# Two ScalarE passes that convert weights: the first writes float32 into the weight's own tile instead of bfloat16 into the raw one

## Chip, cores and metric

One core of one Trainium2 chip. The metric is the device time of the core in microseconds (us); the kernel before took a median of 1000.03 us in three runs (998.05 to 1000.8).

The engines are named as in the profile: PE (TensorE matmul), PEld (its weight load), DVE (VectorE), ACT (ScalarE), POOL (GpSimd), SP (SyncE, which here issues every DMA). Each engine works through its own instructions in order.

## The reference

Pooled attention, then a gated feed-forward block over the 4608 tokens:

```python
k_p = k.reshape(B, H, S // 8, 8, D).mean(axis=3)        # B = H = 8, S = 576, D = 64
v_p = v.reshape(B, H, S // 8, 8, D).mean(axis=3)
attn = softmax(q @ k_p.T / sqrt(D))                     # 1e-9 added to each sum
x = (attn @ v_p).transpose(0, 2, 1, 3).reshape(B * S, H * D)
xn = x / sqrt(mean(x * x) + 1e-6) * rms_g
g = xn @ w_gate                                         # 512 -> 1536
out = (g * sigmoid(g) * (xn @ w_val)) @ w_out           # 1536 -> 512
```

The three weight matrices reach the kernel as 64-bit words (float64 values seen as int64), and the kernel makes float32 of them on the chip.

## The kernel before

**Shape of the work.** The tokens go in nine blocks of 512. The first three blocks are multiplied plainly (`mm1`, `mm2`; tiles `psg` and `po` in the profile); the later six go in pairs through a scheme with seven products of halves instead of eight (`pxy`, `pf`), whose weight blocks and sums of blocks were stored to DRAM (`blocks`, `sum`, `vB`, `vs`) in the first part and are loaded back for each pair. Every operand is split into a high part and a low part in fp32r, so that each product takes three matmuls. Attention for a batch (`pss` scores, `pst` turned probabilities, `psx` result) runs ahead of the block that needs it.

**Order.** One table of steps, `ORDER`, fixes the order of the instructions on all engines: a step is a name of one or two letters and its indices, `:` is followed by the PSUM banks that it takes, `/` by the numbers of the slots that it takes in a pool with several slots. Steps with an underscore belong to the first part (batches 0 and 1 and block 0). Nothing is rearranged after that.

**The conversion.** The weights come in 26 chunks, ten of 1024 words a partition and sixteen of 512. Each chunk passes these steps, whose letters stand in `ORDER`:
- `l` (`w_load`, L321): a DMA from DRAM to a raw tile `wx`, moved by three bytes, so that byte 4 of each 8 is the double's top byte (sign and seven exponent bits) and the 32-bit word at byte 0 holds the bits below it.
- `a` (`w_bend`, L327, ACT): a Prelu with a bias, which reads that byte as int8 at every eighth byte and writes bfloat16 at bytes 4 and 5 of the same eight, in `wx` itself.
- `b` (`w_top`, L336, ACT): takes the chunk's own tile `wt` (for the 512 chunks a slot of the tag `out`, 0 or 1; for the 1024 chunks a region of the weights' space), reads the bfloat16 at every eighth byte, and writes int32 densely into `wt`: the sign and the top of the exponent in float32's place. Two Prelus in a row give the function with two bends that the exponent needs.
- `c` (`w_join`, L340, DVE): shifts the word at byte 0 of each eight and ORs it into `wt`, which is then the float32 weight. It is the last reader of `wx`.
- `h` (`w_hi`, L354, ACT) rounds `wt` to the high part, `w` or `W` (`w_lo`, L305, DVE or POOL) subtracts it for the low part. This is the last reader of `wt`.

The slots `out` 0 and 1 are shared: besides the `wt` of the 512 chunks they hold the tiles that `wh` and `wl` fill (L781, L785) and `ws` stores (L789), and later results on their way out.

**Who else uses ACT at that time.** All exponentials (L451, L509), most copies from PSUM (L552, L554, L593, L600), Silu (L1047), the high parts of the activations (L1085), and a table load of 1.28 us at each change between Exp, Silu and Sqrt.

Of the kernel before, what the change touches and what calls it, by code (L numbers as in the profile page):

```python
# [15 lines left out]
BF16 = mybir.dt.bfloat16  # L16
# [59 lines left out]
_bb/1 _B01:6 _h8 _H01 _cb _m103 _u1 wf01 Wf02 _E111 _w8 _G1 _m113 _F1 wh03/0 Wl03 _la _X100 _hb _Wb _lf/0 Wf03 ws03
_e2:0 _o0:7564 _aa _g2:3 _i1/1 _ba _ca _L1 wh02/1 _o1 wl02 _af _u2 _G2 _R111 _bf/0 _cf _F2 _N110 _Q10 wd0 _i2/1
_T110:2/1 _D110 _hf _Wf _j2 _ha _g3:1 _lc _q12 _e3:0 wh01/0 _V11/0 _u3 _G3 _wa ws02 _o2 _N111 _F3 _ac _bc _cc _k13
_i3/0 _lh/0 _ah _hc _g4 _T112:1 _bh/1 _D112 _j3 _T111:3 _le _D111 _e4:0 _ch _u4 _hh wl01 ws01 Wt1/0 wh04/0 _ae Wl04
_Wc Wf10 _S12:32 _lg _Wh Wf11 Wf12 wf13 _be _M120 _M121 ws04 _G4 _F4 wh11/1 wl11 _ce _A110:1 _v20/1 _V20/1 _Y110 ws11  # L80
_o3 _A111:1 wh13/0 wd1 _i4/0 Wt2/1 _E120 _g5:0 wh14/1 _R120 Wl14 ws14 Wf20 _li Wl13 _L4 ws13 _ag _o4 _bg _e6 _he _We
Wf21 _u5 _cg _E121 _R121 wf22 _N121 wh12/1 Wl12 _e5:2 ws12 _G5 _Y111 _T121:1/1 Wf23 _F5 _i5/0 wh23/0 _v12 _j5 _N120
_D121 Wl23 wh21/1 Wl21 _q13 _K13/1 _T122 _ai _bi _ll/0 _hg ws23 ws21 _Wg _g6 _u6 _V12/0 _D122 _lk _k20 _v13 _o5 _G6
wh22/1 _F6 _i6/1 _ci _S13:10 _M130 _T120:3 wh24/0 Wl24 _D120 _j6 wl22 _M131 _g7 _u7 _hi ws22 _e7 _ak _o6 _K20/1 _bk
_ck _G7 _F7 ws24 _E130 _A121:3 _al _bl/1 _cl _ln/1 _an _bn/0 _cn _i7/1 _R130 _E131 _R131 _N131 _A120:2 _Y120 _hn _Wn
_j7 _Y121 _g8:1 _u8 _V13/0 _G8 _wi _N130 wd4 _e8:0 _F8 _hl _wl _lj/0 _aj _bj/0 _cj _lm/1 _am _bm/1 _T131:1/1 _o7 _D131
_hk _T130 _D130 _q20 sc20:21 wd2 _Q11/0 _cm _T132 _D132 _Wk _hj _A130:3 _Y130 Wt3/1 Wf30 _A131 _Y131 Wf31 lv21/0
# [169 lines left out]
def body(ctx: ExitStack, tc: tile.TileContext, qT, kT, vN, w1, w2, gain, out, outT):  # L257
# [51 lines left out]
    def w_load(n):  # L309
# [910 lines left out]
```

## Time and profile before

| what | value |
|---|---|
| median of three runs | 1000.03 us |
| profiled execution, its own time | 998.13 us |
| its span, first to last instruction | 996.4 us |
| PE busy | 956.7 us, 96% of the span |
| DVE, ACT, POOL busy | 666.6, 540.6, 482.6 us |
| conversion passes on ACT (L327, L336), all before 193 us | 26 and 26 instructions |
| DMA | 211.40 MB, mean 212 GB/s |

PE is busy nearly all the time, so the span is PE's work plus PE's idle time. The tenths of busy time in 40 slices (24.9 us each) show where the idle time lies, and the line of the granted clock where PE worked at a lower clock; the timeline of an engine tells, in brackets, how long it was idle before a piece of work and which engine, tile and line ended the wait. The chain that ended last is given to 69% to PE, 5% to POOL and 3% each to DVE, ACT and DMA.

### The profile page before, as it was taken

Reading aid. Unit: us, or ns where it says so; the run is one execution under the profiler, and the core shown is the slowest. Engines: PE = TensorE matmul, PEld = TensorE weight load, DVE = VectorE, ACT = ScalarE, POOL = GpSimd, SP = SyncE. Lnnn points to the kernel's source line nnn. Section 1 sums busy time; section 2 is a strip of 40 time slices with the busy share of each in tenths; the row PEclk is TensorE's granted clock in tenths of the full one; section 3 lists DMA queues with packets and bytes.
Section 4 is the critical chain, followed back from the end, with each engine's and each line's share of the span. In section 5 each row is a group of like instructions: output and inputs, shape, how many; then the busy total and the mean of one; then the engine's idle time right before and its main releaser. Section 6 shows DMA issues by size and latency. Waiting matters only on the chain.

```text
span 996.4 us, 14144 instructions
## 1 busy us (share of the span) xinstructions
PE 956.7 (96%) x4670; PEld 758.5 (76%) x4670; DVE 666.6 (67%) x1084; ACT 540.6 (54%) x955; POOL 482.6 (48%) x618
## 2 busy tenths in 40 slices
PE   7777988999999999999999999999999999999998
PEld 7466766877777787777777777878778778888886
DVE  6435756788889689878877868746566785442433
ACT  6899989854564655755446455541534552212332
POOL 3324543711231323442335688741276896245786
PEclk7579999999999999999999999999999999999999
DMA  9425666566667756977978776657786575766646
GB/s 290 154 99 174 232 228 183 189 203 202 199 212 216 221 146 195 302 238 230 291 223 270 217 234 219 215 188 250 237 275 188 159 235 171 219 212 206 215 142 208
DMA packets 142296, 211.40 MB, mean 212 GB/s; under 512 B 12240, under 2 KB 78288, under 8 KB 142224
## 3 DMA queue, kind: packets, MB, share of 16 engines
q1 hardware_dynamic: 142224, 210.51, 68.0%
q8 instruction: 37, 0.61, 0.3%
q14 instruction: 35, 0.29, 0.1%
HBM read 154.23 MB, written 56.23 MB: 211 GB/s over the span
## 4 chain that ended last, share of the span: by engine, by line
PE 69%; POOL 5%; DVE 3%; ACT 3%; DMA 3%; issue 1%; SPq 0%; DVEq 0%; ACTq 0%
PE pxy L905 30%; PE pf L985 14%; PE psg L1069 13%; PE po L1103 6%; PE psx L570 3%; PE pss L488 3%; POOL fp L305 2%; POOL xp L305 1%; DMA wp<-blocks 1%; ACT wx L327 1%; DMA pt<-rows 1%; DMA out<-o 1%; POOL w L305 1%; DVE xraw L654 0%; ACT wt L336 0%
## 5 line engine op out<-in xcount | busy, mean ns | idle before, releaser
L905 PE MATMUL pxy<-xp,wp 128*128 128x512 f32 x1512 | 361.2, 391 | 1.7 <-ACT o L1114 0.8
L905 PEld LDWEIGHTS pxy<-xp,wp 128*128 128x128 f32 x1512 | 282.4, 188 | 65.5 <-issue 2.9
L985 PE MATMUL pf<-fp,ring 128*128 128x512 f32 x756 | 189.6, 393 | 1.8 <-DVE fu L305 0.8
L1069 PE MATMUL psg<-xh,w 128*128 128x512 f32 x544 | 172.4, 399 | 6.8 <-ACT prob L451 6.1
L985 PEld LDWEIGHTS pf<-fp,ring 128*128 128x128 f32 x756 | 139.7, 188 | 38.0 <-issue 2.7
L1069 PEld LDWEIGHTS psg<-xh,w 128*128 128x128 f32 x544 | 101.9, 191 | 32.6 <-ACT prob L451 7.4
L1069 PE MATMUL psg<-xl,w 128*128 128x512 f32 x272 | 107.1, 394 | 0.0
L305 POOL TENSOR_TENSOR hl<-act,hh 128x256 fp32r<-128x256 f32 x58 | 46.9, 830 | 115.8 <-ACT hh L1085 94.6
L305 POOL TENSOR_TENSOR fp<-fs,fp 128x256 fp32r<-128x256 f32 x108 | 81.1, 777 | 41.0 <-ACT fp L958 37.2
L305 POOL TENSOR_TENSOR fp<-act,fp 128x256 fp32r<-128x256 f32 x72 | 55.0, 785 | 82.3 <-ACT fp L958 81.0
L305 POOL TENSOR_TENSOR w<-wt,w 128x256 fp32r<-128x256 f32 x50 | 43.2, 892 | 73.8 <-ACT w L354 73.8
L1103 PE MATMUL po<-w,hh 128*128 128x512 f32 x288 | 74.0, 394 | 0.0
L1103 PEld LDWEIGHTS po<-w,hh 128*128 128x128 f32 x288 | 55.1, 191 | 11.9
L305 POOL TENSOR_TENSOR fp<-hb,fp 128x256 fp32r<-128x256 f32 x68 | 54.5, 827 | 13.6 <-ACT fp L958 13.6
L1069 PEld LDWEIGHTS psg<-xl,w 128*128 128x128 f32 x272 | 51.7, 190 | 11.3
L1164 ACT COPY hb<-pxy 128x512 f32<-128x512 f32 x36 | 21.0, 587 | 72.1 <-PE pxy L905 72.1
L340 DVE SCALAR_TENSOR_TENSOR wt<-wx,wt 128x512 uint32<-128x512 uint32 (+1 forms) x26 | 23.5, 908 | 48.0 <-ACT wt L336 46.1
L958 ACT CAST fp<-act 128x512 fp32r<-128x512 f32 x36 | 22.2, 619 | 58.3 <-DVE act L1172 49.0
L958 ACT CAST fp<-fs 128x512 fp32r<-128x512 f32 x54 | 33.1, 618 | 34.6 <-POOL fs L305 17.5
L327 ACT ACTIVATE wx<-wx,shift 128x512 bf16<-128x512 int8 (+1 forms) x26 | 48.9, 1893 | 4.7 <-DMA wx<-w 4.7
L1171 DVE TENSOR_TENSOR u<-u,pxy 128x512 f32<-128x512 f32 x36 | 24.7, 685 | 39.7 <-PE pxy L905 39.5
L305 POOL TENSOR_TENSOR fs<-act,hb 128x256 f32<-128x256 f32 x32 | 23.3, 751 | 50.4 <-DVE act L1172 28.0
(194 smaller groups left out, 1634.0 us busy)
## 6 DMA issues: line engine op xcount, KB each, us to landing
wp<-sum SPq DMA_DIRECT2D x144, 256.0 KB
wp<-blocks SPq DMA_DIRECT2D x108, 256.0 KB
ring<-vs SPq DMA_DIRECT2D x72, 256.0 KB
ring<-vB SPq DMA_DIRECT2D x54, 256.0 KB
sum<-wt SPq DMA_DIRECT2D x48, 256.0 KB
blocks<-w SPq DMA_DIRECT2D x24, 512.0 KB
wx<-w SPq DMA_DIRECT2D x10, 1023.6 KB
v<-vN SPq DMA_DIRECT2D x32, 288.0 KB
```

The source lines that it names most:

```text
L305: getattr(eng, op)(*(x[..., o:o + step] for x in (out, a, b)))
L327: nc.scalar.activation(u, z, AF.Prelu, bias=shift[:, 0:1], alpha=SMALL)
L340: nc.vector.scalar_tensor_tensor(u, raw["x", n][0], 5, u, ALU.logical_shift_right, ALU.bitwise_or)
L488: nc.tensor.matmul(s["ps", h][:, t * SP:(t + 1) * SP], s["q"][r, o:o + P], s["pk"][r, :], start=True, stop=True)
L570: nc.tensor.matmul(ps[r, :n], s["pv"][:, r], x, start=True, stop=True)
L905: nc.tensor.matmul(ps[:, :NB], w[:, a, c, :], x[:, b, c, :], start=j == 0 and not more, stop=j == len(todo) - 1, skip_group_check=more)
L958: nc.scalar.copy(y[:, 0], f_source(i, k, j))
L985: nc.tensor.matmul(ps[c], w[:, a, c * P:(c + 1) * P], x[:, b], start=j == 0 and n == 0 and not more, stop=j == HALF - 1 and n == 2, skip_g ...
L1069: nc.tensor.matmul(ps[:, :NB], w[:, c, cols], x[c], start=(j == 0), stop=(j == len(todo) - 1))
L1103: nc.tensor.matmul(po[i][t], x[i, f][:, t * P:(t + 1) * P], w, start=(f == 0 and k == 0), stop=(f == NF - 1 and k == 2))
L1164: cp=lambda i, f: S_.copy(later(i, f), st["XY", i, f, 0]),
L1171: v1=lambda i, f: V.tensor_add(u2(i, f), u2(i, f), st["XY", i, f, 5]),
```

## The change

The first pass `w_bend` now takes the chunk's own tile `wt` and writes float32 densely into it; the second pass `w_top` reads this float32 and writes int32 in place, over it. The raw tile is only read. With the tile, the slot number (`/0`, `/1`) moves in `ORDER` from `b` to `a`, sixteen times; the table has the same 3289 steps in the same order (its lines are broken elsewhere, which is why all of it stands in the diff). The numbers of lines after the passes are smaller by five.

```diff
-_zg:6 _q00 _q02 _l5/0 _k00 _K00 _S00:16 _a5 _b5/0 _c5 _k02 _K02 _S02:24 _M001 _M000 _U001 _E000 _M021 _M020 _U021 _k01
+_zg:6 _q00 _q02 _l5/0 _k00 _K00 _S00:16 _a5/0 _b5 _c5 _k02 _K02 _S02:24 _M001 _M000 _U001 _E000 _M021 _M020 _U021 _k01
...
-        raw["x", n] = x[:, :, 0], x.bitcast(I8)[:, :, 4], x.bitcast(BF16)[:, :, 2]
+        raw["x", n] = x[:, :, 0], x.bitcast(I8)[:, :, 4]
...
     def w_bend(n):
-        _, z, u = raw["x", n]
-        nc.scalar.activation(u, z, AF.Prelu, bias=shift[:, 0:1], alpha=SMALL)
-
-    def w_top(n):
         f, j = CHUNKS[n]
         if j == 3:
             t = space2(f + 1 if f < 3 else NF - 1 - f % 2, [P, 2 * WC], F32, f"wt{n}")
         else:
             t = two([P, WC], F32, tag="out", name=f"wt{n}")
         raw["t", n] = t
-        nc.scalar.activation(t.bitcast(I32), raw["x", n][2], AF.Prelu, scale=UNIT, bias=shift[:, 1:2], alpha=1.0 / SMALL)
+        nc.scalar.activation(t, raw["x", n][1], AF.Prelu, bias=shift[:, 0:1], alpha=SMALL)
+
+    def w_top(n):
+        t = raw["t", n]
+        nc.scalar.activation(t.bitcast(I32), t, AF.Prelu, scale=UNIT, bias=shift[:, 1:2], alpha=1.0 / SMALL)
```

No instruction changes its place on any engine. What moves is the wait for `wt`'s slot: from the second pass to the first. Two places on ACT show it. The first is near 23 us, chunks 1 and 0 (L327 is the first pass, L336 before and L331 now the second). Before:

```order
L327 ACTIVATE wx_242<-wx_242,shift 128x512 [waits DMAHW4_49]
L327 ACTIVATE wx_242<-wx_242,shift 128x512 [waits DMAHW7_49]
L449 ACTIVATE early<-early 128x5 [waits DVE_49]
L451 ACTIVATE prob,early<-pss_0_0_275,early 128x72 [waits PE_49,Activation_49,Pool_49]
L451 ACTIVATE prob,early<-pss_0_0_275,early 128x72 x4
L453 ACTIVATE early<-early,tiny 128x5 [waits Activation_49]
L336 ACTIVATE wt_305<-wx_242,shift 128x512
L554 COPY own_139<-pst_2_2_309 72x2x64 [waits PE_49]
L336 ACTIVATE wt_313<-wx_242,shift 128x512 [waits Pool_49]
```

Now:

```order
L327 ACTIVATE wt_271<-wx_242,shift 128x512 [waits DMAHW4_49]
L327 ACTIVATE wt_273<-wx_242,shift 128x512 [waits DMAHW7_49,Pool_49]
L444 ACTIVATE early<-early 128x5 [waits DVE_49]
L446 ACTIVATE prob,early<-pss_0_0_277,early 128x72 [waits PE_49,Activation_49]
L446 ACTIVATE prob,early<-pss_0_0_277,early 128x72 x4
L448 ACTIVATE early<-early,tiny 128x5 [waits Activation_49]
L331 ACTIVATE wt_271<-wt_271,shift 128x512
L549 COPY own_139<-pst_2_2_310 72x2x64 [waits PE_49]
L331 ACTIVATE wt_273<-wt_273,shift 128x512
```

The wait for POOL, which ends its subtraction from the slot's last tenant, stands ahead of the exponentials now and behind them before.

The second place is near 163 us, the first passes of chunks 19 and 22, with the copies of turned probabilities (`pt`) behind them. Before:

```order
L354 CAST w_9_1372<-wt_1303 128x512 [waits DMAHW5_49,DVE_49]
L327 ACTIVATE wx_1375<-wx_1375,shift 128x512 [waits DMAHW3_49]
L336 ACTIVATE wt_1378<-wx_1375,shift 128x512 [waits Activation_49,Pool_49]
L327 ACTIVATE wx_1381<-wx_1381,shift 128x512 [waits DMAHW4_49]
L336 ACTIVATE wt_1384<-wx_1381,shift 128x512 [waits DVE_49,Activation_49]
L552 COPY pt_3_1386<-pst_3_1_1387 72x512 [waits PE_49]
```

Now:

```order
L349 CAST w_9_1372<-wt_1302 128x512 [waits DMAHW5_49,DVE_49]
L327 ACTIVATE wt_1377<-wx_1375,shift 128x512 [waits DMAHW3_49,Activation_49,Pool_49]
L331 ACTIVATE wt_1377<-wt_1377,shift 128x512 [waits Activation_49]
L327 ACTIVATE wt_1383<-wx_1381,shift 128x512 [waits DMAHW4_49,DVE_49]
L331 ACTIVATE wt_1383<-wt_1383,shift 128x512 [waits Activation_49]
L547 COPY pt_3_1386<-pst_3_1_1387 72x512 [waits PE_49]
```

Here too the waits for POOL and DVE moved up by one instruction, from the second pass of a chunk to its first.

## Rows read from the trace of the kernel before

**Rows 1.** The page: busy tenths and granted clock in 40 equal slices.

```profile
PE   7777988999999999999999999999999999999998
ACT  6899989854564655755446455541534552212332
PEclk7579999999999999999999999999999999999999
```

**Rows 2.** Busy time by stretch: us, PE, PEld, DVE, ACT, POOL, PEclk, DMA share, GB/s.

```profile
200.00:996.40 796.40, 786.88 (x3804) 626.11 (x3802) 550.02 (x891) 368.77 (x612) 397.88 (x510) 1.00 0.71 217
```

**Rows 3.** ACT's groups up to 200 us, by shape: busy us, mean ns, idle before.

```profile
L327 ACT ACTIVATE wx<-wx,shift 128x1024 bf16<-128x1024 int8 x10 | 26.1, 2607 | 0.0
L327 ACT ACTIVATE wx<-wx,shift 128x512 bf16<-128x512 int8 x16 | 22.9, 1446 | 4.7 <-DMA wx<-w 4.7
L336 ACT ACTIVATE wt<-wx,shift 128x512 int32<-128x512 bf16 x16 | 12.1, 757 | 0.5
L336 ACT ACTIVATE wt<-wx,shift 128x1024 int32<-128x1024 bf16 x10 | 12.1, 1209 | 0.3
```

**Rows 4.** ACT's timeline: start us, length us, instruction.

```profile
29.64 2.58 ACT L327 ACTIVATE wx<-wx,shift 128x1024 bf16<-128x1024 int8 x1
31.97 0.68 ACT L552 COPY own<-pst 72x512 f32<-72x512 f32 x1
...
81.55 1.19 ACT L336 ACTIVATE wt<-wx,shift 128x1024 int32<-128x1024 bf16 x1
82.64 0.61 ACT L1085 CAST hh<-act 128x512 fp32r<-128x512 f32 x1
83.15 1.45 ACT L327 ACTIVATE wx<-wx,shift 128x512 bf16<-128x512 int8 x1
84.69 0.77 ACT L336 ACTIVATE wt<-wx,shift 128x512 int32<-128x512 bf16 x1
```

**Rows 5.** Line L327 alone by stretch: us, ACT busy (count), PEclk, DMA.

```profile
20.00:41.00 21.00, 6.59 (x4) 0.50 0.58 175
41.00:56.00 15.00, 5.40 (x3) 0.73 0.50 177
...
67.00:88.30 21.30, 5.56 (x3) 0.97 0.21 78
...
119.00:130.00 11.00, 2.62 (x1) 0.99 0.85 262
130.00:135.00 5.00, 0.00 (x0) 0.68 0.54 151
135.00:160.00 25.00, 8.10 (x4) 1.00 0.70 224
```

**Rows 6.** PE's timeline where it had been idle: idle us and releaser in brackets.

```profile
32.02 1.07 PE L546 MATMUL pst<-ident,main 128*72 128x128 f32 x4 [2.16 <-POOL main L478]
...
38.40 1.23 PE L570 MATMUL psx<-own 72*64 72x288 f32 x4 [1.50 <-ACT own L552]
...
55.91 1.23 PE L570 MATMUL psx<-own 72*64 72x288 f32 x4 [5.97 <-ACT own L600]
...
88.30 1.60 PE L1103 MATMUL po<-w,hl 128*128 128x512 f32 x4 [4.60 <-ACT prob L451]
...
129.91 1.22 PE L1069 MATMUL psg<-xh,w 128*128 128x512 f32 x2 [2.38 <-ACT prob L451]
...
141.94 1.33 PE L488 MATMUL pss<-pk,q 64*128 64x72 f32 x18 [0.55 <-ACT pt L554]
...
159.87 0.73 PE L1069 MATMUL psg<-xh,w 128*128 128x512 f32 x2 [3.74 <-ACT prob L451]
```

**Rows 7.** ACT's timeline: a wait for PE, and a first pass near 163 us.

```profile
66.86 0.58 ACT L552 COPY pt<-pst 72x512 f32<-72x512 f32 x1 [1.76 <-PE pst L546]
...
163.62 1.48 ACT L327 ACTIVATE wx<-wx,shift 128x512 bf16<-128x512 int8 x1
```

**Rows 8.** POOL's timeline near 161 us: a subtraction of two pieces.

```profile
161.56 3.04 POOL L305 TENSOR_TENSOR w<-wt,w 128x256 fp32r<-128x256 f32 x2
```

More of the change, by code (lines that the diff above doesn't have):

```diff
@@ L15 @@
 U8 = mybir.dt.uint8
-BF16 = mybir.dt.bfloat16
 AF = mybir.ActivationFunctionType
@@ L234 @@
[L234 to L236 removed]
+_zg:6 _q00 _q02 _l5/0 _k00 _K00 _S00:16 _a5/0 _b5 _c5 _k02 _K02 _S02:24 _M001 _M000 _U001 _E000 _M021 _M020 _U021 _k01
+_O021 _K01 _f _k03 _v03 _V03 _I021 _K03 _R000 _O001 _q01 _I001 _h5 _N000 _N001 _S01:10 _M010 _k10 _M011 _U011 _E020 _N021
@@ new lines @@
+xc400 lq42 sc42:03 me26:2 gt26 rc31 whb2/0 mx420/1 sb420 wsb1 ex420 whb3/1 dm41 rs31 vl26 Wlb3 mx421/1 sb421 mo25 av401:1
+ft301 sm420/0 xd40 hi26/0 Lo26 ex421 sm421/0 Wlb2 lq43 sc43:32 mx431/0 xc401 dp41/1 av411 xd41 mx430/1 xc411 av410:1
+xc410 lv42/1 wsb3 pv42/0 Wfb3 whb4/1 mg27:0 gt27 Nm421 Nm420 Wlb4 tr42/0 sb431 ex431 lk50 pk50/1 sb430 lv43/1 pv43/1
+sm431/1 ex430 sm430/1 me27:1 zt40/1 Nm430 zt41 vl27 Nm431 me28:0 mo26 dm42 sq40 lq50 tr43/0 wsb2 hi27/1 wsb4 Zf40 Zf41
+Lo27 zh41/1 Zl41 ft311 dp42/1 Zf42 Zf43 mg28:3 sc50:12 mx501/1 dm43 zh43/0 gt28 vl28 zl43 zs43 sb501 yh31 zs41 yl31
@@ new lines @@
+ys35 yh35 zh54/1 pr310 rl315/3 Zl54 cp31 mo2b pr312 lk52 pk52/0 rl304/1 yh34 Yl34 rl302/4 ev22/0 pr302 rl321/2 lv50/1
+sb511 sa31 ex511 st22 zs54 yl32 Yl35 pr320:0 pr304:4 ev21/0 pr315:7 rl301/7 sb510 sa30 rl311/4 sm511/0 pv50/0 ev20/1
+rl313/6 ex510 rl314/0 sm510/0 Nm510 pr301:6 u230 st21 st20 ev23/0 ys36 pr303 u330 pr313:1 c230 pr311:5 rl305/1 pr305:6
+yh36 zh51/1 pr314 Yl36 rl325/5 u231 Zl51 rl333/6 pr325 u331 c231 v231 lq52 v230 pr321:4 rl316/4 Nm511 sw30 vb30 pr316
+dp50/1 sw31 vb31 rm41:1 rl306/3 v131 rt41 rl324/7 va31 pr306 v130 sc52:25 va30 Fs310 fh300/5 Fl300 rl323/4 tr51/0 cp32
@@ new lines @@
+pm321 pr386 sw38 rl396/3 vb38 Fs332 rl394/7 pr394:0 fh332/4 rs50 Fs341 v138 xc611 sa38 Nm621 ft330 rl393/4 pr393:6 u339
+c239 sw39 rl3a3/1 Fl332 tr62/0 pr395:1 v239 lq63 rl392/6 pr392 av610:7 xc610 lv63/1 sq60 Fs342 pv63/0 ft331 sc63:20
+mx631/1 va38 rl3a1/2 fh322/7 dm62 rl3a4/7 mx630/1 pm330:76 sb631 ft332 _J10 sb630 rl3a5/0 sa39 pr396 v139 va39 pm331
+ex631 Fl322 dp62/0 Fs362 sm631/0 fh323/5 rl3b2/3 fh340/8 ft322 Nm631 pr3a0:0 cp3a vb39 pr3a3:2 rl3b0/5 Fs333 ex630
+sm630/0 Fs343 pr3a1:1 fh333/6 pr3a4:3 Fl333 pm322 Fs363 sq61/0 pm332 Nm630 tr63/1 Fl323 dm63 u23a u33a c23a sw3a Fl340
@@ new lines @@
+fh342/7 pr3a5:1 v23a vb3a av620:2 pr3b0:3 cp3b rl3a2/7 pr3a2 ft334 xc620 Fs344 pr3b2 yh50 lk71 pk71/1 Jn61 ft333 pm333
+rl3a6/2 pr3a6 v13a rl3b1/6 sa3a ft323 ft324 va3a Fs334 fh334/3 av621:2 fh324/4 xd62 yh51 xc621 pm323 Fl334 rl3b3/4
+pr3b3:0 sa3b Fl342 Fl324 dp63/1 yl50 av631:1 xd63 xc631 yl51 fh343/5 av630:2 pm324 sq62/0 Jn62 pr3b1 fh351/6 rl506/1
+rl3b4/5 zs51 Fl343 u23b rl500/3 xc630 pr3b4:1 rl3b6/0 pm334 rl3b5/2 pr3b5:2 sq63/0 fh341/4 Jn63 sh6/1 u33b c23b v23b sw3b
+Fl351 Fs364 vb3b ft340 pm340:10 fh344/3 fs335 Sl6 Fl341 rl510/5 lq70 pr3b6 v13b va3b rm60:3 rt60 rc60 ft341 rs60 pm341
@@ new lines @@
+fh360/3 oe30 rl523/6 Fl354 ys56 sw50 Qd30 yh56 Yl56 qf30/0 fh362/5 rl514/3 Fl360 lv70/1 u351 pr514:4 Nm701 c251 ft354
+sw51 qf31/1 v250 pv70/1 lq71 pm354 rl515/0 pr515 v251 ft355 rl520/2 pm355 qg31 ex700 ft360 rl524/3 sm700/1 qg30 pr520:4
+Nm700 pr506 v150 cp52 rl530/7 va50 rl516/0 pr523:5 Fl362 Fl363 pr516 pm360 v151 fh500/4 tr70/0 ft361 rl525/1 rl526/6
+pr521:2 u252 vb50 u352 rl522/5 pr524:7 c252 ft362 pr522 fh361/8 Fl361 pr525 v252 sc71:75 va51 mx711/0 rl531/2 mx710/1
+pm361 rm61:2 Fl500 sb711 ex711 pm362 Fs510 fh364/7 dm70 fh510/8 sb710 pr526 v152 ex710 rl533/4 ft363 pm363 rl534/5
@@ new lines @@
+pr586 ft531 dp72/0 av720:3 v158 rl594/5 va58 pr594:7 ft530 of30 fh522/7 Fs542 pv73/1 lq73 av721:6 xc721 rl5a0/7 xd72
+sc73:10 fh532/8 rl593/1 mx731/1 pr593:6 xc720 sb731 ex731 mx730/0 sb730 ex730 Fl550 u359 c259 pr5a0:3 Fl532 Fs562 rl5a2/4
+rl5a3/6 pr5a3:1 sm730/1 fh531/6 Fl531 Fl522 pm521 rl5b4/5 sm731/1 Nm731 rl5b1/1 pr595:7 v259 pr5a1:0 sw59 vb59 cp5a
+rl596/7 pr596 v159 rl592/6 ft522 Fs533 rl5a4/7 pm522 rl5b0/0 u25a u35a pm530 pr592 pr5a2 fs561 ft532 Fs543 fh543/4 sq72/1
+Fl543 Nm730 rl5a5/2 tr73/0 dm73 sa5a ft524 pr5a4:0 fh533/7 c25a pm531 pr5a5:1 Jn72 pr5b0:3 pr5b1:0 Fl533 sa59 va59
@@ new lines @@
+rl5a6/3 pm532 ft523 ft533 v25a pr5a6 fh523/6 Fl523 pm533 sw5a vb5a cp5b Fs544 u25b Fs534 dp73/0 av730:2 fh542/8 Fl542
+fh534/5 v15a rl5b6/1 av731:1 xd73 Fs563 pm523 rl5b2/6 fh541/7 Fl541 va5a xc731 xc730 sq73/0 Jn73 Fl534 rl5b3/0 fh524/6
+pr5b3:1 u35b pr5b4:0 ft534 sh7/0 sl7 rl5b5/2 Fl524 c25b ft543 sw5b pr5b5:2 v25b vb5b fs535 rm71:1 ft542 rm70 pm524 rt71
+ft540 pr5b2 fh540/6 rc71 rt70 sa5b pm534 rc70 Fl540 ft541 Fs545 pr5b6 fh544/5 pm540:30 Fl544 v15b va5b pm541 fh525/6
+pm542 rs70 pm543 ft544 pm544 rl710/0 rs71 fh535/8 rl702/2 ys73/10 yh70 Fl525 fh551/7 ft525 pm525 Fl535 Fs565 fh545/4
@@ new lines @@
+pm710:76 rl766/2 pr766 rl762/5 pr762 ft704 rl790/4 v176 og51 sw76 rl780/3 rl781/1 Fs715 pm704 vb76 Fs730 Fs740 fh713/7
+ft712 Fl713 rl772/0 pm711 ft713 pr780:1 pr790:0 ft705 cp78 Fl712 pm712 sa76 va76 fh714/6 pr781:2 fh720/3 u278 pm713 Fl720
+rl773/6 pr772 ft714 pr773:2 pm705 rl782/3 pr782 ft715 rl784/7 fh715/8 Fl714 qa70 pm714 u377 sa77 rl774/2 pr774 ft720
+fh740/4 rl775/0 qa71 c277 pr775 v277 Fl715 pm715 qb70 Fl740 rl783/1 rl776/4 pr776 v177 sw77 vb77 rl793/2 pm720 cp79
+rl785/5 pr784 ft721 fh730/8 Fl730 va77 rl794/0 pr783:7 u378 rl792/4 Fs731 ft730 c278 qb71 sw78 Fs760 fh721/7 Fs741
@@ L237 @@
+qg70 fh761/8 fh762/5 ft761 Fl761 ft762 fh763/4 Fl763 Fl762 fh764/6 pm761 ft764 ft763 ft765 qg71 Fl764 og70 og71 oe71
+pm762 pm763 fh765/7 Fl765 pm764 of70 pm765 qh70 qh71 oh70 oh71
 """
```

293 lines of the change are left out of this document (123 added, 170 removed).

## The prediction, made before the changed kernel was run

> **What bounds the kernel now.** I read the 40 slices first. PE stands at 9 from the eighth slice to the last but one; the only sevens and eights, and the only granted clock below 9, are in the first seven slices, up to some 174 us; ACT stands at 8 and 9 in six of those seven [rows 1]. The stretch from 200 us on confirms it: PE is busy 786.88 of 796.40 us at a clock of 1.00, ACT 368.77 [rows 2]. Past 200 us the time is PE's own work and at most 9.5 us can be gained there; a change to ACT's weight conversion, which ends at 193 us, pays only as far as it closes PE's holes before 200 us.
>
> Next I read those holes from PE's timeline [rows 6]. Seven are of interest: 2.16 us before 32.02 (released by POOL), 1.50 before 38.40, 5.97 before 55.91, 4.60 before 88.30, 2.38 before 129.91, 0.55 before 141.94 and 3.74 before 159.87, these six released by ACT. Together 20.9 us, 18.7 of them ended by ACT. So ACT is the bound in that part, and the question is how much ACT time the change takes out ahead of each hole.
>
> **Part 1: the first pass (L327).** It takes 1446 ns for 512 elements and 2607 for 1024, 49 us in all for 26 instructions; the second pass, the same function with the same kind of bias, takes 757 and 1209 [rows 3]. Both read one element in every eight bytes. They differ in two things: the first reads int8 instead of bfloat16, and writes two bytes in every eight where the second writes densely. The second pass's row thus clears the stepped read of the charge, at least for two-byte elements. What is left is the stepped two-byte write, which the change removes, or the int8 read, which it keeps. No row of before shows an int8 read with a dense write, so I bound it: from above by today's 1446 and 2607 (the read is the cost, gain nothing), from below by a plain dense float32 pass, 0.61 us for 512 [rows 4]. I take the second pass's 757 and 1209, because that row has the function, the step and the dense four-byte write, and differs in the type read alone.
>
> A saving on ACT is the distance from one start to the next, not the duration. A first pass of 1024 holds the next independent instruction back by 31.97 - 29.64 = 2.33 us, a second pass by 82.64 - 81.55 = 1.09 [rows 4]; the saving is 1.24. For 512 I take off the same overlaps, 0.25 and 0.10: 1.20 against 0.66, a saving of 0.54. Where its own second pass follows at once it has to wait for the end (83.15 to 84.69 [rows 4]), and the saving is the difference of the durations, 0.69 and 1.40.
>
> The Trainium skill, ScalarE: Activation LUTs, section What ACT_TABLE_LOAD costs, says that an ACTIVATE with a bias operand takes 280 ns plus 0.833 ns for each element whatever the function, 706 ns for 512 as an estimate from that page. The second pass's 757 agrees with it, the first pass's 1446 doesn't; by the page alone the first pass would have nothing to lose, by the row it has 0.69 us to lose.
>
> **Part 2: the second pass.** It reads dense float32 instead of stepped bfloat16. Between 757 now and 0.61 us for the plain dense pass [rows 3, 4] there is at most 0.15 us to gain each; I take nothing. That it works in place costs nothing that I can see, since DVE's join and this pass keep their places in the order.
>
> **Part 3: what reaches PE.** The counts come from L327's rows by stretch [rows 5], the holes from PE's timeline [rows 6]. I carry the shift along:
> - 20 to 41 us: four first passes, three of 512 and one of 1024, 3 x 0.54 + 1.24 = 2.9 on ACT. The hole at 32.02 is ended by POOL, behind the first two only (1.1); the rest can only come out of the 1.50 before 38.40. So between 1.1 and 2.6; I take 1.9.
> - 41 to 56: three, one of 512 with its second pass behind it, one of 1024, one of 512: 0.69 + 1.24 + 0.54 = 2.5. The hole of 5.97 is larger. Shift 4.4.
> - 56 to 67: one of 1024. ACT has to wait 1.76 us for PE at 66.86 [rows 7], so this saving makes that wait longer. Nothing.
> - 67 to 88.3: two of 512, one of 1024 that ends before a table load: 0.54 + 1.40 + 0.69 = 2.6, less than the hole of 4.60. Shift 7.0.
> - 88.3 to 130: PE works through from 88.30 to 127.5, so only what lies close to the hole counts. One of 1024 (1.40) runs in the last eleven us. The hole is 2.38; with what earlier passes leave over I take 2.0. Shift 9.0.
> - 135 to 160: two of 1024 and two of 512, all with their second passes behind them: 2 x 1.40 + 2 x 0.69 = 4.2, against holes of 0.55 + 3.74 = 4.3. Shift 13.2.
> - 160 to 200: four of 512, no hole of PE behind them. Nothing.
>
> **Part 4: the wait that moves.** The first pass now needs the slot `out` that the second needed before. ACT works in order, so behind a first pass that waits stand the copies and exponentials for PE. The worst place that the rows show is chunk 19's: POOL subtracts from the slot's last tenant until 161.56 + 3.04 = 164.60 and the first pass starts at 163.62 [rows 7, 8]. It would wait 1.0 us, about as much as it and its neighbour save; PE has no ACT hole there, and I charge 0.2.
>
> **Part 5: the clock.** After the 2.38 us hole two matmuls took 1.22 us, after the 3.74 us hole another two 0.73 [rows 6], and in the 5 us from 130 the granted clock was 0.68 [rows 5], between the levels 1.2 and 2.4 GHz: 5 x 0.32 = 1.6 us of work lost. If that hole and the last one close, 0 to 3.2 us come on top (an estimate from that one row, twice). I leave it out of the sum and put it into the range.
>
> **The sum.** 13.2 - 0.2 = 13. The profiled execution took 998.13 us and would take 985. The median of the runs is 1.9 us above it; I carry that along: 1000.03 - 13 = 987.0 us.
>
> **The rivals.**
> A. *The int8 read is the cost.* Then L327 stays at 1446 and 2607, ACT saves nothing, and no hole of PE closes. For it: no other row reads int8, and the type is one of two differences. Against it: a read of one byte fetches less than a read of two at the same step, and that one is fast. Time: 1000, or 1001 with the wait of 1.0 us. The Trainium skill, SBUF — State Buffer, section Specifications (TRN2), wants two accesses in each line of 16 bytes for full bandwidth. A step of eight bytes has two, in the write as in the read; by that rule the stepped write is no culprit, and A is what is left. The second pass's read agrees with it; for a write no row here shows it.
>
> B. *Half of it.* The read takes part of the cost, or ACT's savings are lost to DVE, POOL or a load that is then late. Some 6 us, 994. It counts as faster.
>
> C. *Slower: ACT stands at the slots.* If the first pass stays slow (A) and the subtractions on POOL keep the slots, the moved wait is all that changes. Where two pieces on POOL take 3.04 us [rows 8], the price was 1.0 us at one place. It decides from three such places on, since 3 us are what can be told from no change, and it needs them ahead of PE's holes; at four, 1000 + 4 = 1004.
>
> **How the numbers follow.** A measurement of this kernel can tell about 0.3%, 3 us, from no change. My forecast with B stands for 0.80: the writing side is the only difference between the passes besides the type read. A has 0.14, C 0.06. Faster by over 0.3% is then 0.80, within 0.3% 0.14, slower 0.06. The range: all holes and the clock, 13.2 + 3.2 and some of the two holes left over, give 979 at the low end; at the high end B is taken in and A's edge, 999. Outside are most of A and C, under 0.2.
>
> **What would show it.** In the profile of the changed kernel: L327's groups at about 757 and 1209 ns, ACT's busy time down by some 25 us before 200 us, the second pass unchanged. PE's holes before 129.91, 141.94 and 159.87 gone, those before 55.91 and 88.30 shorter by some 2.5 us each, and the stretch behind as long as before. I am wrong if L327 keeps its means (A), if the first passes are preceded by idle time put down to POOL or to a store (C), or if L327 is short and the holes still stand with another releaser (B).

## The result, and the profile after

The changed kernel took a median of 984.12 us (983.23 to 986.13, four runs) where the kernel before, measured beside it, took 1000.41 us (998.05 to 1001.72, four runs). The ratio is 0.9842, with a 95% interval from 0.9818 to 0.9867: 16 us saved, where 13 were forecast. The profiled execution took 983.23 us with a span of 981.5 us, 14.9 us less than the span before.

The page of the changed kernel, first its totals, then busy tenths and granted clock in 40 equal slices (24.5 us each); the rows to hold beside it are [rows 1]:

```profile
PE 954.1 (97%) x4670; PEld 756.2 (77%) x4670; DVE 667.8 (68%) x1084; ACT 515.9 (53%) x955; POOL 483.2 (49%) x618
...
PE   7799999999999999999999999999999999999997
...
ACT  6888787745545656565456456242543542213332
PEclk7679999999999999999999999999999999999999
```

PE is at 9 from the third slice on instead of the eighth. ACT's busy time went from 540.6 to 515.9 us, 24.7 us less; PE's idle time went from 996.4 - 956.7 = 39.7 us to 981.5 - 954.1 = 27.4 us. So half of what ACT lost reached PE as idle time: 12.3 us. The other 2.6 us of the span are PE's own busy time, which fell although the number of matmuls is the same.

ACT's groups of the two passes in the changed kernel, up to 200 us, by shape (busy us, mean ns of one, idle before and its releaser), the answer to [rows 3]:

```profile
L327 ACT ACTIVATE wt<-wx,shift 128x1024 f32<-128x1024 int8 x10 | 12.3, 1229 | 1.4 <-DMA wx<-w 1.4
...
L327 ACT ACTIVATE wt<-wx,shift 128x512 f32<-128x512 int8 x16 | 12.0, 758 | 5.6 <-DMA wx<-w 4.7 <-POOL w L300 0.9
L331 ACT ACTIVATE wt<-wt,shift 128x512 int32<-128x512 f32 x16 | 11.5, 721 | 0.3
L331 ACT ACTIVATE wt<-wt,shift 128x1024 int32<-128x1024 f32 x10 | 11.5, 1152 | 0.2
```

The first pass fell from 1446 to 758 ns for 512 elements and from 2607 to 1229 for 1024. The second fell a little too, from 757 to 721 and from 1209 to 1152.

PE's timeline of the changed kernel where PE had been idle (start us, length us, instruction, in brackets the idle time and its releaser), the answer to [rows 6]:

```profile
30.43 1.07 PE L541 MATMUL pst<-ident,main 128*72 128x128 f32 x4 [3.13 <-POOL main L473]
...
37.34 2.29 PE L657 MATMUL psr<-one,own 128*128 128x1 f32 x10 [1.22 <-ACT own L595]
...
49.75 1.23 PE L565 MATMUL psx<-own 72*64 72x288 f32 x4 [2.56 <-ACT own L595]
...
79.57 1.38 PE L1098 MATMUL po<-w,hl 128*128 128x512 f32 x4 [2.10 <-ACT prob L446]
...
118.66 0.74 PE L1064 MATMUL psg<-xh,w 128*128 128x512 f32 x2 [0.39 <-ACT prob L446]
...
144.57 0.74 PE L1064 MATMUL psg<-xh,w 128*128 128x512 f32 x2 [2.08 <-ACT prob L446]
```

The same instructions of before start at 32.02, 40.98, 55.91, 88.30, 129.91 and 159.87 us. They come earlier by 1.59, 3.64, 6.16, 8.73, 11.25 and 15.30 us, and the span ends 14.9 us earlier: the whole gain is there by the last of these events, and 0.4 us of it is given back later.

Where it came from, by the windows between those events (us, then busy us and count of PE, PEld, DVE, ACT, POOL, granted clock, DMA share, GB/s), of the changed kernel:

```profile
0.00:118.66 118.66, 103.59 (x537) 79.99 (x537) 70.61 (x122) 94.62 (x241) 49.09 (x68) 0.80 0.62 209
118.66:144.57 25.91, 23.60 (x122) 18.01 (x122) 15.76 (x23) 22.37 (x52) 8.88 (x10) 1.00 0.81 255
144.57:981.50 836.93, 826.93 (x4012) 658.22 (x4012) 581.47 (x939) 398.95 (x664) 425.24 (x541) 1.00 0.70 215
```

and of the kernel before:

```profile
0.00:129.91 129.91, 104.57 (x536) 80.58 (x536) 70.09 (x122) 111.99 (x241) 48.54 (x68) 0.80 0.58 194
129.91:159.87 29.96, 25.47 (x123) 19.57 (x123) 15.51 (x23) 26.50 (x52) 8.83 (x10) 0.95 0.66 210
159.87:996.40 836.53, 826.70 (x4012) 658.39 (x4012) 581.04 (x939) 402.14 (x664) 425.24 (x541) 1.00 0.70 215
```

To the event at 129.91, 11.25 us are saved, of which 104.57 - 103.59 = 1.0 is PE's busy time and 10.3 its idle time. In the next stage 4.05 us are saved, of which 25.47 - 23.60 = 1.9 us is busy time at the same work, and 2.2 us idle time. Behind that PE's work and time are as before within 0.4 us.

### The profile page after: what moved, and what is told of

The parts are those of the page before. It is cut to its first block, busy times and chain, and to the rows that moved or that the text cites. A ratio compares the mean times of both kernels' runs of the same rounds, so it can differ in the third digit from the quotient of the medians.

```text
span 981.5 us, 14145 instructions
## 1 busy us (share of the span) xinstructions
PE 954.1 (97%) x4670; PEld 756.2 (77%) x4670; DVE 667.8 (68%) x1084; ACT 515.9 (53%) x955; POOL 483.2 (49%) x618
## 4 chain that ended last, share of the span: by engine, by line
PE 77%; ACT 6%; DMA 5%; DVE 3%; issue 3%; POOL 2%; SPq 1%; DVEq 0%; POOLq 0%; ACTq 0%
PE pxy L900 31%; PE pf L980 16%; PE psg L1064 15%; PE po L1098 8%; PE psx L565 3%; PE pss L483 3%; DMA wp<-blocks 2%; POOL w L300 1%; ACT wt L327 1%; ACT wt L331 1%; ACT prob L446 1%; DMA wx<-w 1%; PE psr L657 1%; DMA pt<-rows 1%; DMA ring<-vB 1%
## 5 line engine op out<-in xcount | busy, mean ns | idle before, releaser
L1166 DVE TENSOR_TENSOR u<-u,pxy 128x512 f32<-128x512 f32 x36 | 24.7, 685 | 40.0 <-PE pxy L900 39.8
L1160 DVE TENSOR_TENSOR u<-hb,pxy 128x512 f32<-128x512 f32 x36 | 24.6, 684 | 33.4 <-PE pxy L900 19.4
```

The source lines that it names most:

```text
L1160: u2=lambda i, f: V.tensor_add(u2(i, f), later(i, f), st["XY", i, f, 1]),
L1166: v1=lambda i, f: V.tensor_add(u2(i, f), u2(i, f), st["XY", i, f, 5]),
```

## The experiments

The first question is what made the old first pass slow. The change takes away three things at once: the two-byte type, the step of eight bytes in the write, and the write into the tile that is being read. The theories in the expectations are, in words: any write at a step of eight bytes is slow; any write of a two-byte type is slow, whatever its step; a write into the raw tile is slow; a two-byte write at a step of eight bytes is slow in any tile; and rival A, the int8 read is slow. The verdicts below name them in words.

**Four bytes at every eighth byte, in the raw tile.** This is the kernel before with the type of the write alone changed: float32 at bytes 4 to 7 of each eight.

```diff
-        raw["x", n] = x[:, :, 0], x.bitcast(I8)[:, :, 4], x.bitcast(BF16)[:, :, 2]
+        raw["x", n] = x[:, :, 0], x.bitcast(I8)[:, :, 4], x.bitcast(F32)[:, :, 1]
```

> The kernel before, but the first pass writes float32 (four bytes) at bytes 4 to 7 of every eight of the raw tile, so step and tile are those of before and only the width of the write is another. Theories for what made the first pass take 1446 and 2607 ns: W (a write that fills half of a four-byte word): first pass about 760 and 1230 ns, whole kernel about 984. S (the step of eight bytes in the write): stays at 1446 and 2607, kernel about 1000. T (reading and writing in the same tile): stays, about 1000. B (bfloat16 as output type, wherever it goes): 760 and 1230, about 984.

Measured: 982.58 us, ratio 0.9816 (0.9796 to 0.9836). Its groups on ACT up to 200 us, by shape:

```profile
L327 ACT ACTIVATE wx<-wx,shift 128x1024 f32<-128x1024 int8 x10 | 12.4, 1238 | 0.0
L336 ACT ACTIVATE wt<-wx,shift 128x1024 int32<-128x1024 f32 x10 | 12.3, 1231 | 0.3
...
L336 ACT ACTIVATE wt<-wx,shift 128x512 int32<-128x512 f32 x16 | 12.2, 760 | 0.7 <-POOL w L305 0.2
...
L327 ACT ACTIVATE wx<-wx,shift 128x512 f32<-128x512 int8 x16 | 12.1, 765 | 4.3 <-DMA wx<-w 4.3
```

The step of eight bytes is still there, the tile is still the raw one, the read is still int8, and the pass takes 765 and 1238 ns. So neither the step by itself, nor the tile, nor the int8 read is the cost. What is left has to do with the two bytes. The wait for the slot, too, stands at the second pass again (the releaser POOL is in the row of L336), and the time is that of the changed kernel.

**Two bytes at every fourth byte, in the own tile.** From here on the changed kernel is the base.

```diff
-        nc.scalar.activation(t, raw["x", n][1], AF.Prelu, bias=shift[:, 0:1], alpha=SMALL)
+        u = raw["u", n] = t.bitcast(BF16).rearrange("p (n o) -> p n o", o=2)[:, :, 0]
+        nc.scalar.activation(u, raw["x", n][1], AF.Prelu, bias=shift[:, 0:1], alpha=SMALL)
...
-        nc.scalar.activation(t.bitcast(I32), t, AF.Prelu, scale=UNIT, bias=shift[:, 1:2], alpha=1.0 / SMALL)
+        nc.scalar.activation(t.bitcast(I32), raw["u", n], AF.Prelu, scale=UNIT, bias=shift[:, 1:2], alpha=1.0 / SMALL)
```

> The changed kernel, but the first pass writes bfloat16 into the lower half of every four-byte word of the weight's own tile. W: first pass 1446 and 2607 ns as in the kernel before, kernel about 1000. S: a step of four bytes is half the old one, so below 1446, perhaps 1100, kernel about 992. T: 760, about 984, since nothing is written into the tile that is read. B: 1446, about 1000.

Measured: 987.46 us, ratio 0.9865 (0.9844 to 0.9886). The first pass on ACT, by shape:

```profile
L329 ACT ACTIVATE wt<-wx,shift 128x1024 bf16<-128x1024 int8 x10 | 14.7, 1470 | 1.5 <-DMA wx<-w 1.5
L329 ACT ACTIVATE wt<-wx,shift 128x512 bf16<-128x512 int8 x16 | 13.8, 873 | 6.0 <-DMA wx<-w 5.1 <-POOL w L301 0.9
```

Between the two: 115 ns more than the dense float32 write for 512 elements and 241 for 1024, where the old write at a step of eight cost 688 and 1378 more. The width alone isn't the cost, or this pass would take 1446; the step isn't a plain proportion either. Of what was expected for this pass only "below 1446" was met; it took none of 760, 1100 and 1446 ns.

**Two bytes, dense, in the own tile.** The same edit with the bfloat16 in the upper half of the tile, without gaps.

```diff
+        u = raw["u", n] = t.bitcast(BF16)[:, t.shape[1]:]
```

> The changed kernel, but the first pass writes bfloat16 densely into the upper half of the weight's own tile. W, S and T: 760 and 1230 ns, kernel about 984. B alone: 1446 and 2607, about 1000.

Measured: 985.83 us, ratio 0.9849 (0.9828 to 0.9869).

```profile
L329 ACT ACTIVATE wt<-wx,shift 128x1024 bf16<-128x1024 int8 x10 | 12.2, 1217 | 1.6 <-DMA wx<-w 1.6
...
L329 ACT ACTIVATE wt<-wx,shift 128x512 bf16<-128x512 int8 x16 | 12.0, 754 | 6.7 <-DMA wx<-w 5.8 <-POOL w L301 0.9
...
L333 ACT ACTIVATE wt<-wt,shift 128x512 int32<-128x512 bf16 x16 | 11.5, 722 | 0.3
```

Dense bfloat16 costs what dense float32 costs, 754 against 758 ns. So a two-byte type by itself is refuted as the cause: it takes the two bytes and the gap together. The second pass takes 722 ns from dense bfloat16, as from dense float32 (721); the 36 ns that it lost against [rows 3] are the price of reading at a step of eight bytes, which the first run shows again with float32 (760).

**The old write in another tile.** To the changed kernel I added, for the ten chunks of 1024, one more pass of 512 elements that writes bfloat16 at every eighth byte of the chunk's own tile, just before the first pass writes over it. It is work that the result doesn't need.

```diff
+        if j == 3:
+            v = t.bitcast(BF16).rearrange("p (n o) -> p n o", o=4)[:, :, 2]
+            nc.scalar.activation(v, raw["x", n][1][:, :WC], AF.Prelu, bias=shift[:, 0:1], alpha=SMALL)
         nc.scalar.activation(t, raw["x", n][1], AF.Prelu, bias=shift[:, 0:1], alpha=SMALL)
```

> The changed kernel with one more pass ahead of the first pass of each of the ten 1024 chunks: 512 of its int8 values are turned into bfloat16 at every eighth byte of the weight's own tile, which the first pass then overwrites. This measures the write of before, apart from the raw tile. U (a two-byte write at a step of eight bytes costs in any tile): 1446 ns, as in the kernel before. R (it costs so much only because it goes into the lines that the same instruction reads): 760 to 873 ns, as with a dense write or a step of four. The whole kernel, with ten more passes on ACT: 5 to 12 us above the changed one; that time is not the point.

Measured: 992.65 us in its one run, and on ACT:

```profile
L330 ACT ACTIVATE wt<-wx,shift 128x512 bf16<-128x512 int8 x10 | 14.6, 1459 | 0.3 <-POOL w L301 0.3
```

1459 ns in a tile that is not read in the same instruction, against 1446 in the raw tile. The price goes with the write of two bytes in every eight, wherever it lands; that the pass read and wrote one tile had no part in it. Of the 14.6 us that ACT worked more, 8.5 us came through to the time (992.65 against the median of 984.12).

**ACT's time given back.** The second question is whether ACT's shorter time is all that counts, or also the place of the moved wait. Here the changed kernel makes each first pass twice, so that ACT has its old time again in the new order.

```diff
+        for _ in range(2):
+            nc.scalar.activation(t, raw["x", n][1], AF.Prelu, bias=shift[:, 0:1], alpha=SMALL)
```

> The changed kernel with every first pass done twice over (the same result), so that ACT has its old load of time again (two passes of 512 hold the next instruction back by 2 x 0.66 = 1.32 us against 1.20 before, two of 1024 by 2 x 1.14 = 2.28 against 2.33) while everything else of the change stays. If the gain is ACT time ahead of PE's holes: 1000 us, plus or minus 2, and the holes before the events at 55.91, 88.30, 129.91 and 159.87 are back. If the gain came another way (the raw tile no longer written, slots, transfers): 984 to 987.

Measured: 1004.83 us (1002.64 to 1005.32), ratio 1.0037 (1.0022 to 1.0051), above the expected 1000 by more than its margin. PE's timeline where it had been idle, beside which [rows 6] are to be held:

```profile
56.14 1.23 PE L566 MATMUL psx<-own 72*64 72x288 f32 x4 [5.59 <-ACT own L596]
88.50 2.05 PE L1099 MATMUL po<-w,hl 128*128 128x512 f32 x4 [4.54 <-ACT prob L447]
129.94 0.73 PE L1065 MATMUL psg<-xh,w 128*128 128x512 f32 x2 [1.94 <-ACT prob L447]
...
159.80 1.22 PE L1065 MATMUL psg<-xh,w 128*128 128x512 f32 x2 [3.97 <-ACT prob L447]
```

The holes are back, and the events stand where they stood before to within 0.3 us. So up to 160 us ACT's time explains the gain, and the order with the moved wait adds nothing that can be seen. The excess lies behind. One event that both traces have, at 200.63 us before, comes at 201.92 here; from there to the end it takes 798.98 us against 795.77, at the same busy time of PE (786.63 and 786.70). PE's waits in that stretch (line waited for, us in total, times, longest us) are, of this run, the two that grew most

```profile
PE pf L981 <- DMA ring<-vs: 2.0, 3, 1.6
PE pxy L901 <- DMA wp<-sum: 1.2, 1, 1.2
```

where the kernel before waits 0.3 us for `ring<-vs` and less than that for `wp<-sum`. These are loads of what the first part stored. Why they come later in this run is not settled.

**The early and the late chunks apart.** The third question is the sum by stages. In one kernel the nine chunks 5, 1, 0, 2, 3, 7, 4, 13 and 6, the first in the order, get the new first pass and the others keep the old one; in a second kernel it is the other way round.

```diff
+NEW = (5, 1, 0, 2, 3, 7, 4, 13, 6)
...
-        nc.scalar.activation(t, raw["x", n][1], AF.Prelu, bias=shift[:, 0:1], alpha=SMALL)
+        u = raw["u", n] = t if n in NEW else raw["x", n][2]
+        nc.scalar.activation(u, raw["x", n][1], AF.Prelu, bias=shift[:, 0:1], alpha=SMALL)
```

Expected of the early ones:

> The change in nine chunks alone, those whose first pass runs before 67 us (5, 1, 0, 2, 3, 7, 4, 13, 6); the other seventeen write bfloat16 into the raw tile as before. If the gain is made hole by hole and carried to the end: the 6.2 us that the event at 55.91 came earlier, so about 994. If an early gain is given back at the later holes: 999 to 1000.

and of the late ones, with the other seventeen numbers in `NEW`:

> The change in the other seventeen chunks. Hole by hole: what the events at 88.30, 129.91 and 159.87 gained after 55.91, 15.3 - 6.2 = 9.1 us, so about 991; with the early half it adds up to the whole. If the later gain needs the early one (holes that close only together): 995 or more, and the two halves don't add up.

Measured: 994.91 us, ratio 0.9939 (0.9917 to 0.9960), and 991.35 us, ratio 0.9918 (0.9897 to 0.9938). PE's timeline of the early kernel:

```profile
82.08 1.86 PE L1101 MATMUL po<-w,hl 128*128 128x512 f32 x4 [4.59 <-ACT prob L449]
...
152.21 1.22 PE L1067 MATMUL psg<-xh,w 128*128 128x512 f32 x2 [3.74 <-ACT prob L449]
```

and of the late one:

```profile
56.45 1.23 PE L568 MATMUL psx<-own 72*64 72x288 f32 x4 [5.28 <-ACT own L598]
...
148.71 0.73 PE L1067 MATMUL psg<-xh,w 128*128 128x512 f32 x2 [1.18 <-ACT prob L449]
```

With the early chunks alone the last event comes 159.87 - 152.21 = 7.7 us earlier, and the holes of 4.6 and 3.74 us that the later chunks cause stand in full. With the late chunks alone the hole before 55.91 is nearly as it was (5.28), the later ones shrink, and the last event comes 11.2 us earlier. The two gains are 0.61% and 0.82%, together 1.43%, against 1.58% for the whole: they add up within the intervals. The early gain is carried from stage to stage, as the prediction carried it: the events at 55.91, 88.30 and 129.91 come at 49.73, 82.08 and 123.71, each 6.2 us earlier. Event by event the halves do not add up, though. At the last one they have gained 7.7 and 11.2 us, where the whole change gains 15.3, and both give some of it back: from there to the end they take 837.79 and 841.89 us, against 836.53 before. In the late kernel PE waits there for loads of stored blocks (line waited for, us in total, times, longest us),

```profile
PE pxy L903 <- DMA wp<-blocks: 3.5, 5, 0.9
```

where the kernel before waits 0.4 us for them. Why these loads come late is not settled here either.

**The last hole.** The changed kernel leaves 2.56, 2.10 and 2.08 us of holes that end with ACT. I tried whether an order that is made for the shorter passes takes them out: three steps of ACT moved ahead, the squares for the norm (`_Z20`, L595) and two steps of exponentials (`_E111`, `_E131`, L446).

```diff
 _Z21
+_Z20
...
-_Z20
 _bd
...
 _L0
+_E111
...
-_E111
 _w8
...
 _A121:3
+_E131
...
-_E131
 _R131
```

> The changed kernel with three steps earlier in the table, so that ACT does what PE waits for before it converts on: Z20 right behind Z21 (the hole of 2.56 us before 49.75 in the changed kernel), E111 right behind L0 (the hole of 2.10 before 79.57), E131 right behind A121 (the hole of 2.08 before 144.57). If ACT's order is what leaves these holes: 6.7 us less and some clock, 974 to 979. If the conversions that come later then end the holes through DVE and POOL: 981 to 985, with other releasers.

Measured: 988.08 us (987.32 to 989.93), ratio 0.9883 (0.9868 to 0.9898): slower than the changed kernel by some 4 us, and outside both expectations. Its PE timeline where PE had been idle:

```profile
79.13 0.97 PE L930 MATMUL po<-w,hl 128*128 128x512 f32 x3 [2.55 <-DVE act L870]
...
139.14 0.72 PE L896 MATMUL psg<-xh,w 128*128 128x512 f32 x2 [0.24 <-ACT prob L278]
146.71 0.60 PE L373 MATMUL pst<-ident,prob 128*72 128x128 f32 x4 [1.82 <-DVE act L870]
```

The event that ends the last hole came at 139.14 us, 5.4 us earlier, with 0.24 us of idle time before it. But what the exponentials passed was late in turn: conversions, of two chunks here and of one before 79.13. ACT's timeline has the second passes of the two at

```profile
142.18 0.72 ACT L163 ACTIVATE wt<-wt,shift 128x512 int32<-128x512 f32 x1
...
143.60 0.72 ACT L163 ACTIVATE wt<-wt,shift 128x512 int32<-128x512 f32 x1
```

DVE, which works in order, stood idle for 5.55 us before its join at 143.00 us, for which the trace names no releaser but which ends when the first of them has ended (142.90), and for 0.66 us before the next join at 144.35. Its product `act` (L870) came behind both, at 145.88, and with it ends PE's new hole before 146.71. The hole before 79.13 ends in the same way. In the 20 us behind the event PE was busy 8.18 and 7.29 of 10 us, where the changed kernel has 9.90 and 9.94 behind its own. The first matmul of the first pair starts at 419.2 us against 415.2, so 4.0 of the 6.6 us by which the span of this execution is longer (988.1 against 981.5) are lost by then, and the rest later; how the loss is shared among the new holes and the loads was not settled. These three moves don't take ACT's holes out: something else that PE needs soon stands behind what they put first.

**The wait that moved, weighed.** Last, the changed kernel and the one with float32 in the raw tile were timed together once more. They differ in where the wait for the slot stands, in 39 and 79 ns for each second pass (760 and 1231 ns against 721 and 1152) and in 7 and 9 ns for each first pass.

> The changed kernel once more, beside the next one on the same chip: 984 us, ratio to the kernel before 0.984.

> The kernel before with float32 in place of bfloat16 in the raw tile, once more. Against the changed kernel it has the waits for the slots and stores at the second pass, as before (a gain of up to 0.9 + 1.4 us, which ACT waited for POOL and for a load near 149 and 133 us in the changed kernel, if that reaches PE), and second passes that are slower by 39 and 79 ns (a loss of 16 x 0.039 + 10 x 0.079 = 1.4 us of ACT). If the moved wait costs something: 1 to 2 us less than the changed kernel. If not: equal to it or up to 1 us more.

Measured: 983.53 us, ratio 0.9833 (0.9806 to 0.9861), and 984.57 us, ratio 0.9832 (0.9806 to 0.9858). There is no difference that can be told. A third slot for chunk 19 alone, which would take its wait away, wasn't tried. No version beat the changed kernel clearly.

## Why the prediction was right, and where its steps were not

**The bound and the place of the gain** were right. All the gain is on PE by the event at 159.87 before, PE's work behind it is the same, and giving ACT its old time back puts the holes back to within 0.5 us.

**Part 1** was right in its sizes: 758 and 1229 ns against 757 and 1209. Its reason was right too, but wider than what holds. It charged the stepped two-byte write, and the runs show that both words are needed: four bytes at a step of eight take 765 ns, two bytes without a step 754, two bytes at a step of four 873, and two at a step of eight 1446 to 1459. It counted two differences between the passes and missed a third, the write into the tile that is being read; the runs clear that one (765 ns for four bytes in the raw tile, 1459 for the old write in another). The second pass's row, from which I took the number, carried 36 ns for its stepped read.

Rival A had a rule beside it: the Trainium skill, SBUF — State Buffer, section Specifications (TRN2), wants two accesses in each line of 16 bytes for full bandwidth. The four-byte write at a step of eight agrees with it (765 against 758 ns dense). The two-byte write, with just as many accesses in a line, doesn't (1446 against 754 dense). The measurement decides: for such a write two accesses in a line are not enough. The Trainium skill, ScalarE: Activation LUTs, section What ACT_TABLE_LOAD costs, gives 280 ns plus 0.833 ns for each element, which makes an estimate of 706 ns for 512. The dense writes are near it (754 and 758), the old one isn't (1446).

**Part 2** charged nothing and had 0.15 us as its bound. The gain was 0.036 and 0.057 us each, 16 x 0.036 + 10 x 0.057 = 1.1 us on ACT in all.

**Part 3**, stage by stage, as increments of the shift: forecast 1.9, 2.5, 2.6, 2.0 and 4.2; measured 3.64, 2.52, 2.57, 2.52 and 4.05.
- The first stage is the term that was mis-sized, 1.9 against 3.64. I took the middle of two bounds, 1.1 and 2.6, from the holes before 32.02 and 38.40 alone. In the trace of the kernel before there are two more that end with ACT beside them,

```profile
35.10 1.23 PE L570 MATMUL psx<-own 72*64 72x288 f32 x4 [0.27 <-ACT own L552]
...
40.98 2.29 PE L662 MATMUL psr<-one,own 128*128 128x1 f32 x10 [1.35 <-ACT own L600]
```

  and in the changed kernel the instructions of 35.10 and 38.40 follow without a hole:

```profile
33.17 1.23 PE L565 MATMUL psx<-own 72*64 72x288 f32 x4
...
34.89 1.23 PE L565 MATMUL psx<-own 72*64 72x288 f32 x4
```

  The event at 32.02 came 1.59 us earlier instead of 1.1, that at 35.10 1.93 and that at 38.40 3.51: the hole of 1.50 closed in full, and the one of 0.27 with it. The hole before 40.98 hardly shrank, from 1.35 to 1.22. It ends with ACT, so the 3.64 is what ACT was ahead by: all of its 2.9 us, 0.39 us by which its first pass starts earlier (22.35 us against 22.74), and some 0.3 us, in part from four slightly shorter second passes. The start of that first pass lies anywhere from 22.05 us (the run with ten more passes) to 23.93 (dense bfloat16) in other executions, so the 0.39 is luck and none of the change's doing.
- From 41 to 88 us both terms were right to 0.03 us, and so was the charge of nothing from 56 to 67. The hole before 55.91 itself shrank by 3.41 us and not by 2.5, since PE needed 0.9 us more for its work ahead of it.
- The stage to 129.91 gave 2.52 instead of 2.0; the hole itself went from 2.38 to 0.39, as forecast.
- The last stage was right in its size, 4.05 against 4.2, and wrong in what it is made of. The holes, with two small ones that end with DVE before and with POOL now, gave 0.19 + 0.55 + 3.74 - 0.24 - 2.08 = 2.16 us, not 4.2, and the last hole, which should have been gone, has 2.08 us left. The other 1.9 us are PE's busy time, most of it the clock of Part 5. That the two together come near 4.2 is luck. One reason that the trace offers why ACT's gain didn't reach the last hole in full is a load, which is rival B on a small scale. ACT's timeline of the changed kernel (start us, length us, instruction, idle time and releaser), the first row there, the second the slot's wait:

```profile
133.14 1.23 ACT L327 ACTIVATE wt<-wx,shift 128x1024 f32<-128x1024 int8 x1 [1.38 <-DMA wx<-w]
...
149.34 0.77 ACT L327 ACTIVATE wt<-wx,shift 128x512 f32<-128x512 int8 x1 [0.92 <-POOL w L300]
```

  ACT, now faster, waited 1.38 us for the raw tile, a wait that the kernel before doesn't have there.

**Part 4** was right to the place and nearly to the size: chunk 19's first pass waits 0.92 us for POOL, 1.0 was worked out. Its price was charged at 0.2, and none is seen.

**Part 5** was left out of the sum and put into the range. In the 5 us behind the two late holes, of the changed kernel:

```profile
118.66:123.66 5.00, 4.76 (x23) 3.57 (x24) 3.20 (x5) 3.90 (x8) 3.75 (x5) 1.00 0.72 227
...
144.57:149.57 5.00, 5.00 (x17) 3.98 (x18) 4.00 (x6) 4.05 (x8) 4.35 (x4) 0.66 0.88 229
```

and of the kernel before:

```profile
129.91:134.91 5.00, 5.00 (x18) 3.95 (x18) 2.36 (x4) 2.79 (x5) 3.69 (x5) 0.67 0.53 148
...
159.87:164.87 5.00, 5.00 (x17) 3.99 (x18) 4.01 (x6) 4.97 (x8) 4.36 (x4) 0.66 1.04 295
```

Behind a hole of 2.38 us the granted clock was 0.67, behind one of 0.39 it is 1.00: 5 x 0.33 = 1.65 us of work that is no longer lost, most of the 1.9 us. Behind the last hole it is 0.66 in both, since 2.08 us of it were left. So one of the two estimates of 1.6 us came in and the other didn't. But the length of the hole is not what decides. In the kernel with the early chunks alone the same hole stands in full,

```profile
123.71 0.73 PE L1067 MATMUL psg<-xh,w 128*128 128x512 f32 x2 [2.39 <-ACT prob L449]
```

and the granted clock of the 5 us behind it was 1.00, the upper level; it was 1.00 behind a hole of 2.24 us in the run with dense bfloat16 and 0.66 behind one of 1.94 in the run with the doubled pass. From 123.71 to its last event the early kernel takes 28.50 us, where the kernel before takes 29.96 with holes of the same length, and that is why it has gained 7.7 us there and not 6.2. That closing the hole brought the clock back is therefore not shown, and the range was the right place for this term.

**The sum** was 13.0; it came out at 14.9 in the profiled executions. The difference is the first stage's 1.7 and the fourth's 0.5, less 0.15 in the last stage and 0.4 given back past 160 us, with the 0.2 of Part 4 not spent. The forecast of 987.0 carried the 1.9 us by which the median of before lay above its profiled execution; for the changed kernel it is 984.12 - 983.23 = 0.9 us, which is the other 1.0 of the 2.9 us between forecast and median.

**The rivals.** A is refuted by every run with an int8 read and a fast pass. C needed A, and it needed three such waits where there is one. B is not refuted as a mechanism: what ACT saved was not all PE's, 24.7 us against 12.3 of idle time.

## What to carry to other kernels

When a pass is slow, look for another pass in the same trace that differs from it in as little as possible: one pair of rows gave the new duration to 2%. Sum such a gain hole by hole on the engine that bounds, and list all the holes of a stage, the small ones too, and look up which engine ends the last one: here that engine's whole saving came through, and the middle of two bounds was the largest error. Keep the slower matmuls behind a hole out of the sum and in the range: the granted clock was 0.67 behind one hole of 2.38 us and 1.00 behind another of 2.39.

## What the runs showed of the hardware that was not expected

ACT's time for a write depends on width and step together. For 512 int8 elements read at every eighth byte, the write took 754 ns as dense bfloat16, 758 as dense float32, 765 as float32 at every eighth byte, 873 as bfloat16 at every fourth byte, and 1446 to 1459 as bfloat16 at every eighth byte. For 1024 it was 1217, 1229, 1238, 1470 and 2607. The prediction had charged step and width as one. A read at every eighth byte costs far less, 757 to 760 ns against 720 to 722 for a dense read or one at every fourth byte. What in the engine or the memory makes the sparse two-byte write so slow no run shows.
